# Decode step of two attention and MLP layers: weights of 448 rows on all 128 partitions, two more K/V slots, last rows in moving form

## The chip, the cores and the metric

The kernel runs on one core of one Trainium2 chip. The metric is the device time of one execution, in microseconds (us). Three runs of the kernel before took 310.23, 316.7 and 318.95 us (median 316.7). The profile below is of one more execution, of 309.65 us.

## The reference

Eight rows x (448 numbers each, one token per batch entry) go through attention, MLP, attention, MLP, each with a layer norm ahead and a residual sum behind. Both rounds use the same weights and the same cache.

```python
W = min(4096, max(256, Sk // 4))                  # 1024 of 4096 positions
q = (layernorm(x) @ wq).reshape(8, 1, 16, 256)    # wq 448 x 4096, 16 heads of 256
k = repeat(k_cache[:, :, Sk - W:, :], 2)          # 8 K/V heads, each for 2 query heads
v = repeat(v_cache[:, :, Sk - W:, :], 2)
o = softmax(q @ k.T * 256 ** -0.5) @ v
x = x + o @ wo                                    # wo 4096 x 448
x = x + silu(layernorm(x) @ w1) @ w2              # w1 448 x 1792, w2 1792 x 448
```

All tensors are bf16. K and V of the window are 67.1 MB, the four weights 10.5 MB (wq and wo 3.67 MB each, w1 and w2 1.61 MB each).

## The kernel before, in words

Everything is loaded once, on SyncE's one DMA queue, in this order: x, wq (four DMAs of 112 rows), the eight K tiles of batch 0, wo, the eight V tiles of batch 0, w1, w2, and then K and V of batch 1, 2 and so on. A K or V tile is 512 KB and fills one of R = 27 slots of SBUF. A batch needs 16 slots and holds them through both layers. A load into a used slot waits on SyncE until layer 2 of an earlier batch has read it; since the queue is in order, all later loads wait behind it.

At the start the eight rows are normalised together and multiplied by wq (L468, 128 matmuls), which gives the queries of layer 1 for all batches. Then the batches go one after the other. Layer 1 of a batch: VectorE transposes each K tile in place (L839, two instructions a tile), TensorE makes scores (L570, four 32-column tiles of the array side by side), VectorE takes maxima (L576) and ScalarE exponentials into e_sb (L590), TensorE turns them (L595) and ScalarE copies them to pT_sb (L599). The values of the first four K/V heads come from pv_rows (L627, V is the moving operand), are copied to o_sb (L634), turned (L636) and scaled (L640). Those of the last four heads come from pv_cols: V is the stationary operand and two columns of pT_sb move (L656, 16 matmuls a head); L662 scales them. wo_part multiplies by wo in four rows of one PSUM bank (L699).

The function chain then does what lies between the two attentions of one batch, for a single row: fold copies the four partial rows to rowb (L713) and turns them into a column (L715), the layer norm sums (L670, L678), the 56 matmuls with w1 (L468), silu (L729 to L738), w2 (L741), fold again, the second norm (L748) and wq (L755), then the query of layer 2 (L760 to L553). The matmuls of L706 multiply by zeros and only keep TensorE occupied. Layer 2 uses the same K and V. While chain runs for batch b, layer 1 of batch b+1 is also being worked on. After the last batch final_wo and final_rows do wo and the last MLP for all eight rows at once (L468 with 8 columns, L781 to L808).

The order of instructions on each engine is not written by hand: every step is a task with a listed duration, and a scheduler (Plan.schedule) places the tasks by the longest chain behind them, with the rates given for the DMAs. Waits follow from the buffers' names: a task waits for the writers of what it reads and for the readers of what it overwrites, and a PSUM bank counts as one buffer.

With 448 = 4 x 112, the weights wq and w1 and the columns of x use partitions 0 to 111 in four chunks. In the second kernel they use three chunks of 128 rows and a last one of 64.

Of the kernel before, what the change touches and what calls it, by code (L numbers as in the profile page):

```python
# [6 lines left out]
BF16 = mybir.dt.bfloat16  # L7
# [245 lines left out]
def bass_interleave_layers__sliding_block_cached__dense_activation_silu__decode_kernel(  # L253
# [12 lines left out]
    CP = D // KC  # L266
# [4 lines left out]
    R = 27  # L271
# [27 lines left out]
    mT = [sb(f"mT{i}", [P, 32], F32) for i in range(2)]  # L299
# [4 lines left out]
    o_sb = [sb(f"o_sb{i}", [P, DH], BF16) for i in range(3)]  # L304
# [37 lines left out]
    C_XF = 256  # L342
    C_W1 = 32
# [33 lines left out]
    dve(lambda e: e.memset(ones_b[:], 1.0), [], ["ones_b"], 0.1, -99)  # L377
    dve(lambda e: e.memset(rowb[:], 0.0), [], ["rowb"], 0.15, -99)
# [4 lines left out]
    dve(lambda e: e.memset(xb0[:, :, NB:NB + 1], 1.0), [], ["xb0_1"], 0.08, -99)  # L383
# [521 lines left out]
```

## Time and profile before

| | |
|---|---|
| profiled execution | 309.65 us |
| its span, first to last instruction | 307.8 us |
| time around the span | 1.85 us |
| busy: TensorE matmul, VectorE, ScalarE, GpSimd | 218.9, 147.1, 69.3, 10.5 us |
| DMA | 77.68 MB, 73% of what the 16 engines' span holds |
[...]

PE is TensorE's matmuls, PEld its weight loads, DVE VectorE, ACT ScalarE, SPq SyncE with its DMA issues. An arrow "bank<-slot,qbd" is output from inputs.

### The profile page before, as it was taken

Reading aid. Unit: us, or ns where it says so; the run is one execution under the profiler, and the core shown is the slowest. Engines: PE = TensorE matmul, PEld = TensorE weight load, DVE = VectorE, ACT = ScalarE, POOL = GpSimd, SP = SyncE. Lnnn points to the kernel's source line nnn. Section 1 sums busy time; section 2 is a strip of 40 time slices with the busy share of each in tenths; the row PEclk is TensorE's granted clock in tenths of the full one; section 3 lists DMA queues with packets and bytes.
Section 4 is the critical chain, followed back from the end, with each engine's and each line's share of the span. In section 5 each row is a group of like instructions: output and inputs, shape, how many; then the busy total and the mean of one; then the engine's idle time right before and its main releaser. Section 6 shows DMA issues by size and latency. Waiting matters only on the chain.

```text
span 307.8 us, 9763 instructions
## 1 busy us (share of the span) xinstructions
PE 218.9 (71%) x4402; PEld 126.5 (41%) x4402; DVE 147.1 (48%) x436; ACT 69.3 (23%) x203; POOL 10.5 (3%) x22
## 2 busy tenths in 40 slices
PE   1052357675798778868796968788878897888683
PEld 1051113433454456345434634554455345443363
DVE  6049400158317934882487269427744674111113
ACT  2000100121312240423132223312231224022111
POOL 0002000000000000010001000000000000000000
PEclk9999999998675999799579999985799579657555
DMA  7999999999995199949955994999099919000000
GB/s 202 292 399 385 372 348 266 333 405 352 372 402 192 21 355 404 317 138 372 402 192 169 377 398 155 308 399 371 21 317 403 365 35 321 5 2 2 0 5 1
DMA packets 49977, 78.30 MB, mean 254 GB/s; under 512 B 2176, under 2 KB 40848, under 8 KB 49488
## 3 DMA queue, kind: packets, MB, share of 16 engines
q1 hardware_dynamic: 49936, 77.68, 73.3%
q8 instruction: 34, 0.56, 0.8%
q14 instruction: 7, 0.06, 0.0%
HBM read 77.67 MB, written 0.01 MB: 252 GB/s over the span
## 4 chain that ended last, share of the span: by engine, by line
PE 53%; DVE 14%; SPq 13%; ACT 10%; DMA 5%; issue 5%; ACTq 0%
PE bank L627 9%; SPq L444 8%; PE bank L468 7%; PE bank L570 6%; PE bank L699 5%; DVE slot L839 5%; PE bank L755 5%; DMA w_sb<-in_B_w_dram 5%; PE bank L656 4%; PE bank L706 4%; PE bank L741 4%; SPq L432 2%; ACT e_sb L590 2%; DVE qbd L553 2%; PE bank L595 2%
## 5 line engine op out<-in xcount | busy, mean ns | idle before, releaser
L839 DVE STREAM_TRANSPOSE slot<-slot 128x512 uint32<-128x512 uint32 x128 | 81.9, 686 | 9.4 <-DMA slot<-in_A_k_cache_dram 9.2
L570 PE MATMUL bank<-slot,qbd 128*8 128x256 bf16 x1024 | 41.0, 300 | 19.6 <-DVE mseg L576 8.9
L570 PEld LDWEIGHTS bank<-slot,qbd 128*8 128x8 bf16 x1024 | 24.7, 90 | 30.9 <-DVE mseg L576 10.1
L627 PE MATMUL bank<-slot,pT_sb 128*2 128x256 bf16 x768 | 30.6, 304 | 6.8 <-DMA slot<-in_A_v_cache_dram 3.9
L706 PE MATMUL bank<-sel,cols_b 128*128 128x480 bf16 x64 | 27.3, 524 | 2.6 <-DVE vneg L729 2.6
L590 ACT ACTIVATE e_sb<-bank,mb 128x256 bf16<-128x256 f32 x32 | 13.4, 471 | 42.9 <-DVE mb L586 42.8
L627 PEld LDWEIGHTS bank<-slot,pT_sb 128*2 128x2 bf16 x768 | 16.6, 88 | 14.8 <-DMA slot<-in_A_v_cache_dram 5.5
L713 ACT ACTIVATE rowb<-bank 128x448 bf16<-128x448 f32 x16 | 8.7, 544 | 61.9 <-PE bank L699 44.8
L699 PE MATMUL bank<-wo_sb,oT 128*1 128x448 bf16 x256 | 21.4, 435 | 1.6 <-issue 0.9
L656 PE MATMUL bank<-pT_sb,slot 128*128 128x2 bf16 x512 | 17.6, 164 | 4.2 <-issue 2.9
L656 PEld LDWEIGHTS bank<-pT_sb,slot 128*128 128x128 bf16 x512 | 15.3, 98 | 12.3 <-issue 9.9
L755 PE MATMUL bank<-wq_sb,xn 112*1 112x512 bf16 x256 | 20.3, 448 | 0.1
L608 DVE TENSOR_REDUCE l_sb<-bank 128x16 f32<-128x64 f32 x16 | 3.6, 225 | 35.0 <-PE bank L603 26.6
L468 PE MATMUL bank<-xbt,w_sb 112*128 112x32 bf16 (+1 forms) x504 | 16.7, 182 | 3.2 <-ACT xbt L722 1.9
L576 DVE TENSOR_REDUCE mseg<-bank 128x1 f32<-128x256 f32 x32 | 13.1, 413 | 11.3 <-PE bank L570 11.3
L662 DVE TENSOR_TENSOR oT<-bank,rl_sb 128x4 bf16<-128x4 f32 x32 | 5.2, 163 | 25.6 <-PE bank L656 25.6
L538 POOL TENSOR_TENSOR qbd<-q1s,mask 128x256 bf16<-128x256 bf16 x16 | 9.8, 613 | 215.4 <-PE bank L570 192.9
L640 DVE TENSOR_TENSOR oT<-bank,rl_sb 128x16 bf16<-128x16 f32 x24 | 5.0, 208 | 25.4 <-PE bank L636 24.8
L468 PEld LDWEIGHTS bank<-xbt,w_sb 112*128 112x128 bf16 x504 | 15.1, 102 | 4.0 <-ACT xbt L722 2.4
L760 ACT ACTIVATE rowb<-bank,rstd 128x512 bf16<-128x512 f32 x16 | 11.0, 687 | 20.1 <-PE bank L755 20.1
L634 ACT ACTIVATE o_sb<-bank 128x256 bf16<-128x256 f32 x24 | 9.2, 384 | 27.5 <-PE bank L627 27.2
L595 PE MATMUL bank<-ident,e_sb 128*128 128x128 bf16 x64 | 7.2, 243 | 11.1 <-ACT e_sb L590 11.1
(117 smaller groups left out, 195.5 us busy)
## 6 DMA issues: line engine op xcount, KB each, us to landing
slot<-in_A_k_cache_dram SPq DMA_DIRECT2D x64, 512.0 KB, 11.0
slot<-in_A_v_cache_dram SPq DMA_DIRECT2D x64, 512.0 KB, 8.6
wq_sb<-in_A_wq_dram SPq DMA_DIRECT2D x4, 896.0 KB, 9.7
wo_sb<-in_A_wo_dram SPq DMA_DIRECT2D x1, 3584.0 KB, 26.9
w_sb<-in_B_w_dram SPq DMA_DIRECT2D x2, 1568.0 KB, 16.4
qbd<-in_A_x_dram SPq DMA_DIRECT2D x1, 7.0 KB
out_dram<-e_sb SPq DMA_DIRECT2D x1, 7.0 KB
```

The costliest lines, as they stand in the source:

```text
L444: dma(lambda e: e.dma_start(slots[s][:, :].rearrange("v (j n) -> v j n", j=4), src.rearrange("j (v uh) d -> v j (uh d)", uh=2)), [("slot", ...
L468: fns.append(lambda e, o=o, i=i: e.matmul(bank[bank_i][:, col + (o - outs[0]) * n:col + (o - outs[0] + 1) * n], lhs(o, i), rhs(i).broadcas ...
L570: fns.append(lambda e, cb=cb, par=par, j=j, kvh=kvh, kv=kv: e.matmul(bank[sc][32 * j:32 * j + 8, k2 * 256:(k2 + 1) * 256], qbd[qi][:, kvh, ...
L576: dve(lambda e: e.tensor_reduce(mseg[layer][:, k2:k2 + 1], bank[sc][:, k2 * 256:(k2 + 1) * 256], AX.X, ALU.max, negate=True), bk(sc), [("m ...
L590: act(lambda e, k2=k2: e.activation(e_sb[ei][:, k2, :, :].rearrange("p uh (jj ul) -> p uh jj ul", ul=4), bank[sc][:, k2 * 256:(k2 + 1) * 2 ...
L595: pe([lambda e, c=c: e.matmul(bank[lb][:].bitcast(BF16)[:, c * P:(c + 1) * P], e_sb[ei][:, c // 2, c % 2, :], ident[:, :], is_transpose=Tr ...
L627: fns.append(lambda e, q=q, uh=uh, j=j, vv=vv: e.matmul(bank[ob][32 * j:32 * j + 2, c0:c0 + DH], pT_sb[ei][:, k2 * 2 + uh, j * 8 + 2 * q:j ...
L656: fns.append(lambda e, a=a, q=q, uh=uh: e.matmul(bank[vb][:, c0 + 2 * a:c0 + 2 * a + 2], vs[:, (2 * q + uh) * DH + a * P:(2 * q + uh) * DH ...
L699: fns.append(lambda e, i=i, c=c, kvh=kvh: e.matmul(bank[XB][32 * c:32 * c + 1, 0:D], oT1[:, i % 2, i // 2:i // 2 + 1], wo_sb[:, i * D:(i + ...
L706: pe([lambda e: e.matmul(bank[YB][:, 32:512], zero_b.broadcast_to([P, P]), sel[:].rearrange("p c m -> p (c m)")[:, 0:480], start=False, st ...
L755: pe([lambda e, j=j, c=c, k2=k2, wb=wb: e.matmul(bank[wb][32 * j:32 * j + 1, :], xn[0:CP, c:c + 1], wq_sb[0:CP, c, (4 * k2 + j) * 512:(4 * ...
L839: dve(lambda e, v=v: e.transpose(v, v), [("slot", s)], [("slot", s)], 0.67, prio, "KT")
```

## The change

It does five things. The names are those of the code.

1. wq and w1 lie on all 128 partitions: three chunks of 128 rows, and the last 64 rows split by columns, the first half of the columns on partitions 0 to 63 and the second half on 64 to 127. wq is loaded by three DMAs of 128 partitions and two of 64, w1 by one of 128 and two of 64. x gets a fifth column (KX = 5): its last 64 numbers stand once on the lower and once on the upper partitions, with zeros on the other half, and x_c picks the column that fits the half. The number of matmuls with weights stays; a fold takes five small matmuls for four.
2. The SBUF that this frees, and some more, goes to two more slots (R = 29). e_sb is one buffer for both layers (two before), and o_sb two for three: both value passes of layer 2 share one.
3. pv_cols moves 32 columns of pT_sb where it moved two; only two of the 32 results are read.
4. final_wo and the last w2 are in moving form: the eight rows are stationary, the weights move with 448 columns in four tiles of the array, and fold8 (a copy on ScalarE and five matmuls) adds and turns the four partial results, twice.
5. The scheduler's DMA rates follow (w1 260 to 350, w2 280 to 350, wq 305 to 400 GB/s).

```diff
-    CP = D // KC
+    CT = D - (KC - 1) * P
+    KX = KC + 1
...
-    R = 27
+    R = 29
...
-    wq_sb = sb("wq_sb", [P, KC, HD], BF16)
-    wo_sb = sb("wo_sb", [P, NCH * D + 16], BF16)
-    w1_sb = sb("w1_sb", [P, KC, F], BF16)
-    w2_sb = sb("w2_sb", [P, FC * D + 16], BF16)
+    wq_sb = sb("wq_sb", [P, 3 * HD + HD // 2], BF16)
+    wo_sb = sb("wo_sb", [P, NCH * D], BF16)
+    w1_sb = sb("w1_sb", [P, 3 * F + F // 2], BF16)
+    w2_sb = sb("w2_sb", [P, FC * D], BF16)
...
-    e_sb = [sb(f"e_sb{i}", [P, 2, 2, P], BF16) for i in range(2)]
-    pT_sb = [sb(f"pT_sb{i}", [P, 4, 32], BF16) for i in range(2)]
+    e_sb = sb("e_sb", [P, 2, 2, P], BF16)
+    pT_sb = [sb(f"pT_sb{i}", [P, 5 - i, 32], BF16) for i in range(2)]
...
-    o_sb = [sb(f"o_sb{i}", [P, DH], BF16) for i in range(3)]
+    o_sb = sb("o_sb", [P, 2, DH], BF16)
...
     def load_wq():
-        for c in range(KC):
-            dma(lambda e, c=c: e.dma_start(wq_sb[0:CP, c, :], A_wq[c * CP:(c + 1) * CP, :]),
-                [("wq", c)], CP * HD * 2, "wq%d" % c, rate=305e3)
+        for c in range(KC - 1):
+            dma(lambda e, c=c: e.dma_start(wq_sb[:, c * HD:(c + 1) * HD], A_wq[c * P:(c + 1) * P, :]),
+                [("wq", c)], P * HD * 2, "wq%d" % c)
+        for h in range(2):
+            dma(lambda e, h=h: e.dma_start(wq_sb[CT * h:CT * h + CT, 3 * HD:],
+                                           A_wq[3 * P:, h * (HD // 2):(h + 1) * (HD // 2)]),
+                [("wq", 3 + h)], CT * HD, "wq%d" % (3 + h))
 
     def load_w1():
-        dma(lambda e: e.dma_start(w1_sb[0:CP, :, :], B_w1.rearrange("(c p) n -> p c n", p=CP)),
-            ["w1"], D * F * 2, "w1", rate=260e3)
+        dma(lambda e: e.dma_start(w1_sb[:, 0:3 * F].rearrange("p (c n) -> p c n", n=F),
+                                  B_w1[0:3 * P, :].rearrange("(c p) n -> p c n", p=P)), [("w1", 0)], 3 * P * F * 2, "w1",
+            rate=350e3)
+        for h in range(2):
+            dma(lambda e, h=h: e.dma_start(w1_sb[CT * h:CT * h + CT, 3 * F:],
+                                           B_w1[3 * P:, h * (F // 2):(h + 1) * (F // 2)]),
+                [("w1", 1 + h)], CT * F, "w1%d" % h)
...
+    def w_l(w, width, o, c, n=P):
+
+        if c < KC - 1:
+            return w[:, c * width + o * n:c * width + (o + 1) * n]
+        o = o * n % (width // 2)
+        return w[:, (KC - 1) * width + o:(KC - 1) * width + o + n]
+
+    def x_c(x, c, h=0):
+
+        return x[:, c] if c < KC - 1 else x[:, c + h]
+
+    def turned(dst, row, m):
+
+        out = [(dst[:, c], row[m, c * P:(c + 1) * P]) for c in range(KC - 1)]
+        return out + [(dst[CT * h:CT * h + CT, KC - 1 + h], row[m, (KC - 1) * P:D]) for h in range(2)]
+
+    def proj(bank_i, col, outs, n_out, w, width, x, n, fresh=True):
 
         fns = []
-        wide = n == 1
-        n = CW if wide else n
         for o in outs:
-            for i in ins:
-                fns.append(lambda e, o=o, i=i: e.matmul(
-                    bank[bank_i][:, col + (o - outs[0]) * n:col + (o - outs[0] + 1) * n], lhs(o, i),
-                    rhs(i).broadcast_to([rhs(i).shape[0], CW]) if wide else rhs(i),
-                    start=(fresh and i == ins[0]), stop=(i == ins[-1]), skip_group_check=not fresh))
+            for c in range(KC):
+                xc = x_c(x, c, 2 * o // n_out)
+                fns.append(lambda e, o=o, c=c, xc=xc: e.matmul(
+                    bank[bank_i][:, col + (o - outs[0]) * n:col + (o - outs[0] + 1) * n], w_l(w, width, o, c),
+                    xc if xc.shape[-1] == n else xc.broadcast_to([P, n]),
+                    start=(fresh and c == 0), stop=(c == KC - 1), skip_group_check=not fresh))
...
-        oi = layer + k2
+        oi = layer
...
-        c0 = (0 if j % 2 == 0 else C_Q) + 4 * j
+        c0 = (0 if j % 2 == 0 else C_Q) + 32 * (j - j % 2)
+        pf = pT_sb[ei][:].rearrange("p c n -> p (c n)")
...
-                        bank[vb][:, c0 + 2 * a:c0 + 2 * a + 2],
+                        bank[vb][:, c0 + 32 * a:c0 + 32 * a + 32],
                         vs[:, (2 * q + uh) * DH + a * P:(2 * q + uh) * DH + (a + 1) * P],
-                        pT_sb[ei][:, k2 * 2 + uh, j * 8 + 2 * q:j * 8 + 2 * q + 2],
+                        pf[:, (2 * k2 + uh) * 32 + 8 * j + 2 * q:(2 * k2 + uh) * 32 + 8 * j + 2 * q + 32],
...
-        pe([lambda e, c=c: e.matmul(bank[YB][0:CP, c:c + 1], rowb[:, c * CP:(c + 1) * CP], ones4,
-                                    start=False, stop=True, skip_group_check=True) for c in range(KC)],
+        pe([lambda e, o=o, r=r: e.matmul(o, r, ones4, start=False, stop=True, skip_group_check=True)
+            for o, r in turned(bank[YB][:, 0:KX].unsqueeze(2), rowb, slice(0, P))],
...
-        dve(lambda e: e.tensor_scalar(xn[0:CP, :], xbt[0:CP, :], nmean[0:CP, 0:1], None, op0=ALU.add),
-            ["xbt", "nmean"], ["xn"], 0.2, prio, "xn")
+        dve(lambda e: e.scalar_tensor_tensor(out=xn[:], in0=xb0[:, :, NB], scalar=nmean[:, 0:1], in1=xbt[:],
+                                             op0=ALU.mult, op1=ALU.add), ["xbt", "nmean"] + XB1, ["xn"], 0.23, prio, "xn")
...
-                bank[wb][32 * j:32 * j + 1, :], xn[0:CP, c:c + 1],
-                wq_sb[0:CP, c, (4 * k2 + j) * 512:(4 * k2 + j + 1) * 512],
-                start=(c == 0), stop=(c == KC - 1), tile_position=(0, 32 * j), skip_group_check=True)
+                bank[wb][32 * j:32 * j + 1, :], x_c(xn[:].unsqueeze(2), c, k2),
+                w_l(wq_sb, HD, 4 * k2 + j, c, 512),
+                start=(c == 0), stop=(c == KC - 1), skip_group_check=True)
...
+    x8 = bank[YB][:, 0:KX * NB].rearrange("p (c b) -> p c b", b=NB)
+
+    def fold8(prio):
+        act(lambda e: e.activation(rowb[:, 0:D], bank[XB][:, 0:D], ACTF.Copy), bk(XB), ["rowb"], 0.54, prio, "rowb8")
+        pe([lambda e, o=o, r=r: e.matmul(o, r, sel8, start=False, stop=True, skip_group_check=True)
+            for o, r in turned(x8, rowb, slice(0, P))], ["rowb", "sel8"], bk(YB), (140, 1), prio, "fold8")
...
-        pe(proj(XB, C_XF, range(KC), range(16 * k2, 16 * k2 + 16), wo_l, lambda i: oT2[:, i % 2, i // 2, :], NB,
-                fresh=False), [(("oT2", b), 2 * h) for b in range(NB) for h in range(4 * k2, 4 * k2 + 4)] + WO_R, bk(XB), (NB, 1), prio, "wo8")
+            pe(lambda e: e.matmul(bank[YB][:, 0:KX * NB], identf, x2s[:].rearrange("p c b -> p (c b)"),
+                                  start=True, stop=True),
+               [("q1s", 0)] + [("x2s", b) for b in range(NB)], bk(YB), (500, 1), prio, "xinit8")
+        pe([lambda e, i=i: e.matmul(
+            bank[XB][32 * (i % 4):32 * (i % 4) + NB, 0:D], oT2[:, i % 2, i // 2, :], wo_sb[:, i * D:(i + 1) * D],
+            start=(i < 4), stop=(i >= NCH - 4), skip_group_check=True) for i in range(16 * k2, 16 * k2 + 16)],
+           [(("oT2", b), 2 * h) for b in range(NB) for h in range(4 * k2, 4 * k2 + 4)] + WO_R, bk(XB), (D, 4), prio,
+           "wo8")
...
-        pe(proj(XB, C_XF, range(KC), range(FC), w2_l, lambda i: hT8[:, i * NB:(i + 1) * NB], NB, fresh=False),
-           H8 + W2_R, bk(XB), (NB, 1), prio + 0.2, "w28")
-        act(lambda e: e.activation(xob[0:CP], xp, ACTF.Copy), bk(XB), ["xbt8"], 0.22, prio + 0.3)
-        ops = bank[YB][:].bitcast(BF16)
-        pe([lambda e, c=c: e.matmul(ops[0:NB, c * CP:(c + 1) * CP], xob[0:CP, c, :], ident[0:CP, 0:CP],
-                                    is_transpose=True, start=True, stop=True) for c in range(KC)],
-           ["xbt8", "ident"], bk(YB), (CP, 1), prio + 0.3)
-        dve(lambda e: e.tensor_copy(orow, ops[0:NB, 0:D]), bk(YB), B8, 0.3, prio + 0.3)
+        pe([lambda e, f=f: e.matmul(
+            bank[XB][32 * (f % 4):32 * (f % 4) + NB, 0:D], hT8[:, f * NB:(f + 1) * NB], w2_sb[:, f * D:(f + 1) * D],
+            start=(f < 4), stop=(f >= FC - 4), skip_group_check=True) for f in range(FC)],
+           H8 + W2_R, bk(XB), (D, 4), prio + 0.2, "w28")
+        fold8(prio + 0.2)
```

## Rows read from the trace of the kernel before

**Rows 1.** The page's chain that ended last, shares of the span by engine
```profile
PE 53%; DVE 14%; SPq 13%; ACT 10%; DMA 5%; issue 5%; ACTq 0%
```
**Rows 2.** Windows: busy us per engine, granted clock, DMA share, GB/s (wq, K, V, w1)
```profile
4.00:14.00 10.00, 0.48 (x12) 0.40 (x12) 3.35 (x21) 0.83 (x3) 0.00 (x0) 1.00 1.02 292
16.00:24.00 8.00, 4.78 (x161) 4.53 (x161) 4.47 (x8) 0.50 (x1) 0.15 (x1) 1.00 1.02 408
...
38.00:46.00 8.00, 3.69 (x58) 1.27 (x62) 0.62 (x4) 0.38 (x1) 0.00 (x0) 1.00 1.09 349
49.00:55.00 6.00, 3.68 (x49) 1.84 (x46) 0.70 (x4) 0.85 (x3) 0.00 (x0) 1.00 1.06 238
```
**Rows 3.** Timeline of the start: start, length, instruction, idle before and releaser
```profile
16.37 3.56 PE L468 MATMUL bank<-xb,wq_sb 112*128 112x9 bf16 x128 [10.80 <-DMA wq_sb<-in_A_wq_dram]
...
56.95 1.68 PE L468 MATMUL bank<-ones_b,w_sb 112*128 112x32 bf16 x56 [2.44 <-DMA w_sb<-in_B_w_dram]
...
61.76 0.96 PE L741 MATMUL bank<-w_sb,hT 128*1 128x448 bf16 x14
```
**Rows 4.** Windows of single stretches; the third number from the right is the granted clock
```profile
143.80:147.20 3.40, 2.60 (x71) 1.72 (x71) 0.67 (x4) 0.00 (x0) 0.00 (x0) 1.00 1.02 401
147.20:157.40 10.20, 8.95 (x117) 4.14 (x118) 6.26 (x15) 2.34 (x7) 0.00 (x0) 0.50 1.04 385
...
177.90:186.60 8.70, 6.54 (x114) 3.61 (x113) 6.47 (x16) 2.58 (x9) 0.00 (x0) 1.00 1.04 386
...
123.30:126.60 3.30, 2.97 (x17) 0.65 (x17) 2.85 (x7) 0.96 (x4) 0.00 (x0) 0.50 1.03 384
...
283.70:307.70 24.00, 14.95 (x362) 10.55 (x362) 5.73 (x22) 3.41 (x11) 0.00 (x0) 0.50 0.01 2
```
**Rows 5.** Groups by line and form: busy us, mean ns, idle before and releasers
```profile
L839 DVE STREAM_TRANSPOSE slot<-slot 128x512 uint32<-128x512 uint32 x128 | 81.9, 686 | 9.4 <-DMA slot<-in_A_k_cache_dram 9.2
...
L656 PE MATMUL bank<-pT_sb,slot 128*128 128x2 bf16 x512 | 17.6, 164 | 4.2 <-issue 2.9 <-DMA slot<-in_A_v_cache_dram 1.0 <-DVE oT L662 0.3
```
**Rows 6.** Timeline: pv_cols' first group and chain's second norm, two of seven batches
```profile
173.74 0.98 PE L656 MATMUL bank<-pT_sb,slot 128*128 128x2 bf16 x32
...
186.30 0.23 DVE L748 TENSOR_SCALAR xn<-xbt,nmean 112x4 bf16<-112x4 bf16 x1
...
261.46 0.73 PE L656 MATMUL bank<-pT_sb,slot 128*128 128x2 bf16 x22
...
276.80 0.23 DVE L748 TENSOR_SCALAR xn<-xbt,nmean 112x4 bf16<-112x4 bf16 x1
```
**Rows 7.** Timeline: w1 matmuls with 32 columns
```profile
180.51 0.85 PE L468 MATMUL bank<-xbt,w_sb 112*128 112x32 bf16 x28
```
**Rows 8.** Timeline of the exponentials and the value copies in one batch
```profile
168.79 0.40 PE L595 MATMUL bank<-ident,e_sb 128*128 128x128 bf16 x4 [1.24 <-ACT e_sb L590]
...
169.40 0.83 ACT L590 ACTIVATE e_sb<-bank,mb 128x256 bf16<-128x256 f32 x2
...
172.66 0.82 ACT L634 ACTIVATE o_sb<-bank 128x256 bf16<-128x256 f32 x2 [1.41 <-PE bank L627]
...
173.05 0.20 PE L636 MATMUL bank<-ident,o_sb 128*128 128x8 bf16 x2
```
**Rows 9.** Timeline of a wo part, a fold and the last rows
```profile
266.21 1.66 PE L699 MATMUL bank<-wo_sb,oT 128*1 128x448 bf16 x16
...
267.92 0.54 ACT L713 ACTIVATE rowb<-bank 128x448 bf16<-128x448 f32 x1 [6.73 <-PE bank L699]
...
269.22 0.17 ACT L722 ACTIVATE xbt<-bank 112x4 bf16<-112x4 f32 x1 [0.76 <-PE bank L715]
...
296.30 1.87 PE L468 MATMUL bank<-oT,wo_sb 128*128 128x8 bf16 x64 [0.32 <-DVE oT L640]
...
303.16 1.65 PE L468 MATMUL bank<-qbd,w_sb 128*128 128x8 bf16 x56 [2.45 <-DVE qbd L799]
```
**Rows 10.** Timeline of VectorE: four K transposes behind the second norm
```profile
186.75 2.48 DVE L839 STREAM_TRANSPOSE slot<-slot 128x512 uint32<-128x512 uint32 x4
```

More of the change, by code (lines that the diff above doesn't have):

```diff
@@ L382, in bass_interleave_layers__sliding_block_cached__dense_activation_silu__decode_kernel @@
         dve(lambda e, q=q: e.memset(ones4[32 * q:32 * q + 1, :], 1.0), [("ones4", 4)], [("ones4", q)], 0.08, -98)
-    dve(lambda e: e.memset(xb0[:, :, NB:NB + 1], 1.0), [], ["xb0_1"], 0.08, -99)
+    dve(lambda e: e.memset(xb0[:, :, NB:NB + 1], 0.0), [], [("xb0_1", 0)], 0.08, -99)
+    for i, (p0, p1, c0, c1) in enumerate(((0, P, 0, KC - 1), (0, CT, KC - 1, KC), (CT, P, KC, KX))):
+        dve(lambda e, p0=p0, p1=p1, c0=c0, c1=c1: e.memset(xb0[p0:p1, c0:c1, NB:NB + 1], 1.0), [("xb0_1", 0)],
+            [("xb0_1", i + 1)], 0.08, -98)
+    XB1 = [("xb0_1", i) for i in range(4)]
     for q in range(4):
@@ L472, in proj @@
         return fns
+    ones_w = ones_c.broadcast_to([P, P])
     def stats8(xp, reads, prio):
-        sq = sq8[0:CP]
-        act(lambda e: e.activation(sq, xp, ACTF.Square), reads, ["sq8"], 0.25, prio)
-        dve(lambda e: e.tensor_copy(sqh8[0:CP, 0], sq), ["sq8"], [("sqh8", 0)], 0.17, prio)
-        dve(lambda e: e.tensor_tensor(sqh8[0:CP, 1], sq, sqh8[0:CP, 0], ALU.subtract),
+        sq = sq8[:]
+        act(lambda e: e.activation(sq, xp, ACTF.Square), reads, ["sq8", "rowb"], 0.25, prio)
+        dve(lambda e: e.tensor_copy(sqh8[:, 0], sq), ["sq8"], [("sqh8", 0)], 0.17, prio)
+        dve(lambda e: e.tensor_tensor(sqh8[:, 1], sq, sqh8[:, 0], ALU.subtract),
@@ L677, in stat_s2 @@
         s1, s2 = bank[bi][:, 0:1], bank[bi][:, 1:2]
-        pe([lambda e, c=c: e.matmul(s2, xbt[0:CP, c:c + 1].broadcast_to([CP, P]), xbt[0:CP, c:c + 1],
+        pe([lambda e, c=c: e.matmul(s2, x_c(x_t, c).broadcast_to([P, P]), x_c(x_t, c),
                                     start=(c == 0), stop=(c == KC - 1)) for c in range(KC)],
@@ L689, in x_init @@
     def x_init(b, prio):
-        pe(lambda e: e.matmul(bank[YB][:, 0:KC], ident[0:CP, :], xb0[0:CP, :, b], start=True, stop=True),
+        pe(lambda e: e.matmul(bank[YB][:, 0:KX], ident[:, :], xb0[:, :, b], start=True, stop=True),
            ["ident", "xb0"], bk(YB), (KC, 1), prio, "xinit")
@@ L704, in keep @@
     def keep(n, prio, after=None):
-        pe([lambda e: e.matmul(bank[YB][:, 32:512], zero_b.broadcast_to([P, P]),
-                               sel[:].rearrange("p c m -> p (c m)")[:, 0:480],
+        pe([lambda e: e.matmul(bank[YB][:, C_W1:512], zero_b.broadcast_to([P, P]),
+                               sel[:].rearrange("p c m -> p (c m)")[:, 0:512 - C_W1],
                                start=False, stop=True, skip_group_check=True) for _ in range(n)],
@@ L725, in chain @@
         for o0, o1 in ((0, 4), (4, 8), (8, 11), (11, 14)):
-            pe(proj(YB, C_W1 + o0 * CW, range(o0, o1), range(KC), w1_l, lambda i: xbt[0:CP, i:i + 1], 1, fresh=False),
+            pe(proj(YB, C_W1 + o0 * CW, range(o0, o1), FC, w1_sb, F, x_t, CW, fresh=False),
                ["xbt"] + W1_R, bk(YB), (CW, 1), prio, "w1")
```

162 lines of the change are left out of this document (74 added, 88 removed).

## Prediction

> **What bounds the kernel now.** I read the chain that ended last first, and look for the engine with the largest share: TensorE has 53%, VectorE and ScalarE 14% and 10%, the DMAs 5% and SyncE 13% [rows 1]. The last two stand together at the start, so there are three stages to price apart. At the start the queue of DMAs is the bound. In the windows of the first 60 us the reader should compare GB/s at a DMA share that is full throughout: wq comes at 292, w1 at 238, but K at 408 and V at 349 [rows 2]. The timeline shows who waits: the first matmuls with wq (10.80 us) and the first with w1 (2.44 us) [rows 3]. In the middle nothing waits for a load. VectorE's K transposes waited 9.4 us for DMAs in all and pv_cols 1.0 us [rows 5], both of it in the start (the first K and V tiles). There each batch costs its own chain through TensorE, VectorE and ScalarE, and the clock matters: stretches of 10 us at 0.50 stand beside others of the same work at 1.00 [rows 4]. The last 24 us run at 0.50 with no DMA to speak of [rows 4]; that is the third stage.
>
> **Loads of wq and w1: -5.0 us.** wq is 3.67 MB, at 292 GB/s 12.6 us [rows 2]. After the change 3.15 MB of it go to 128 partitions with rows of 8 KB, as K's tiles do with 4 KB: at 408 that is 7.7 us. The other 0.52 MB go in two loads to 64 partitions, a shape that the trace does not have. Bounds: 408 (1.3 us) and 238, the slowest load shown (2.2 us). I take 292, since a load to fewer than 128 partitions is nearest to the 112-row wq: 1.8 us. wq saves 12.6 - 9.5 = 3.1 us (2.7 to 3.6). w1 is 1.61 MB: 6.7 us at 238. Its 1.38 MB on 128 partitions come as several pieces a partition, as V does: 349, 3.9 us; the 0.23 MB in halves at 238: 1.0 us. Saved 1.8 us, up to 2.8 at 408 throughout. Sum 4.9, rounded 5.0 (4.5 to 6.4). It all lies on the path: V tiles and w1 queue behind wq without a gap, and the first w1 matmuls start when w1 lands [rows 3]. Three more DMA issues cost nothing while SyncE runs ahead of the wire; where that cover is gone they are three issues of under a microsecond. w2 lands after w1 unchanged; its matmuls start 4.8 us behind the first with w1 [rows 3], which its 1.61 MB at 349 (4.6 us) just fills.
>
> [...] No row here has a 64-partition load.
>
> **pv_cols with 32 columns: -4.0 us.** The instructions cost nothing more: 32 matmuls with two columns take 0.98 us [rows 6], 31 ns each, and the w1 matmuls with 32 columns take 0.85 us for 28, 30 ns [rows 7]. What may change is the clock. It fell while pv_cols and the wo matmuls between them ran in four of the seven batches behind the first: the window 143.80 to 147.20 ran at 1.00, the 10.2 us behind it at 0.50 [rows 4]. The work from pv_cols' first group to the second norm took 12.56 us where no fall came (173.74 to 186.30) and 15.34 in the longest of the seven (261.46 to 276.80) [rows 6]; the four with such a fall took 13.40, 14.74, 14.04 and 15.34, together 7.3 us more than four of the shortest. With 16 times the columns at the same pace the array is busier just there. Against it: right behind the w1 matmuls, which have 32 columns already, the clock held in one batch (177.90 to 186.60) and fell in another, at 0.50 from 123.30 to 126.60 [rows 4]. So a fall may only come some us later. Ends: 0 and -8 (the 7.3, and some of the wq stage that followed at 0.50). I take the half.
>
> **Two more slots: 0.** No transpose or matmul of the middle waits for a load, so earlier loads end no wait. They and the new rates shift the scheduler's order. The nearest price is a group of four K transposes on VectorE, 2.48 us [rows 10], put ahead of or behind something urgent: once, in either direction.
>
> **One e_sb, two o_sb: +0.5 us.** Each adds a wait. e_sb: in the batch shown the second exponentials start at 169.40 and the first layer's turns are over at 169.19 [rows 8], so this wait costs 0 as ordered; queued behind it on ScalarE is the copy of pT. o_sb: the second value copy of layer 2 must now wait until the first is turned. Two copies run back to back at 172.66 for 0.82 us, and the next turn is issued at 173.05 [rows 8]. If that turn is not moved forward, the copy starts behind it (173.25) and not at 172.66 or 173.10, 0.2 to 0.6 us later; with a semaphore each way up to 1.0. pv_cols writes the same PSUM bank that this copy reads, so TensorE's queue, wo included, waits for it. Over seven batches 0 to 7 us. I take 0.5 in all, since a turn can go earlier between the value matmuls.
>
> **Last rows: +1.3 us.** Twice 64 matmuls with wo take 1.87 us each and the 56 with w2 1.65 [rows 9]. In moving form 16 take 1.66 us at 0.50 (L699) [rows 9], 14 at that rate 1.45: saved 0.2 + 0.2 + 0.2. Two folds are new. From the start of rowb to the start of xbt is 1.30 us (267.92 to 269.22) [rows 9], twice 2.6, on the path. Net +2.0 at 0.50. With the clock at 1.00 for part of it, the 46 matmuls would take up to half their time, -2.4, so the ends are -0.4 and +2.0; +1.3 since the stage ran at 0.50 throughout [rows 4]. A fold's fifth matmul, the fifth column of x, the memsets and the other xn instruction are within 0.1 us each.
>
> **Sum.** Against the profiled execution of 309.65: -5.0 - 4.0 + 0 + 0.5 + 1.3 = -7.2, 302.5 us. That execution is the fastest of four; the median run is 7 us above it, about as much as the four falls cost, and I put the spread down to where the clock falls. With half of the falls gone the median should lie some 1.5 above its profile: **304 us**.
>
> **Rivals.** (1) The clock falls as before, only elsewhere. For it speaks the fall at 123.3. Then only -3.2 remains, from the median 316.7: 313.5 us. (2) The clock holds throughout, also at the end: -5.0 - 8 - 0.4 = -13.4 from the profile, 296 us. For it: both neighbours of pv_cols, wo and scores, run at 1.00. (3) Slower: o_sb's wait at its full price. The turn stays behind the second layer's values, pv_cols waits 1.0 us in seven batches (+7), and the clock falls meanwhile as now: -5.0 + 7 + 2.0 = +4.0 from the median, 321 us. It ends on the slower side as soon as the wait costs more than 0.45 us a batch. Against it: the scheduler knows this wait and can move the turn. (4) The change doesn't do what it says: the halves are so slow that wq and w1 gain 1 us or none; with the clock's half 309 us. For it only that no such load is in the trace.
>
> **Chances.** Forecast 0.45, (1) 0.22, (2) 0.13, (3) 0.12, (4) 0.08. A measurement of this kernel can tell about 2% from no change. Faster by over 2% (under 310.4) are the forecast, (2) and a part of (4), 0.62; slower (over 323) a third of (3) and a reordering that goes wrong, 0.09; the rest, 0.29, is within 2%. The range 297 to 314 leaves out (3) and half of (2); the forecast's own is 300 to 309.
>
> **What the profile would show.** The wq matmuls at about 13.3 and not 16.37, w1's at about 52; GB/s near 400 up to wq's end but for a dip. Granted clock 1.00 through the wo matmuls behind pv_cols in most batches, first group to second norm under 13 us. No ScalarE wait on L636 of over 0.3 us ahead of the value copy. Two rowb copies in the last 15 us, and from the first of them to the end some 1 to 2 us more. Wrong would make it: a fall in each batch behind the w1 matmuls; pv_cols waiting for ScalarE; a dip to 200 GB/s that eats the load's gain; K transposes ahead of the queries of layer 2.

## The result, and the profile after

The changed kernel took 288.5 us in the median of its first four runs (285.1 to 294.1), 0.922 of before, with an interval of 0.906 to 0.938; in six more runs (a_again, below) 291.8 us, 0.933 [0.921, 0.945]. All ten together have a median of 291.5 us. The kernel before had 315.0 us over the 66 runs that stand beside the experiments. So the gain is 23.5 us, 7.5%. Forecast were 304 us (297 to 314), which is 12.7 us under the 316.7 us that stood ahead of the prediction. Medians here hold all executions, while the ratios leave out those over 1.5% above the fastest of their kernel, and where too few are left no ratio is given.

The profiled execution took 294.11 us, 15.5 us less than the one profiled before; its span is 292.2 us and its mean granted clock 0.899. First the start, windows of the changed kernel (columns as in rows 2) and its timeline:

```profile
4.00:10.00 6.00, 0.48 (x12) 0.40 (x12) 3.46 (x22) 0.84 (x3) 0.00 (x0) 1.00 1.02 429
11.00:13.00 2.00, 0.00 (x0) 0.00 (x0) 0.00 (x0) 0.00 (x0) 0.00 (x0) 1.00 1.03 231
...
45.00:48.00 3.00, 2.24 (x60) 1.49 (x55) 0.49 (x3) 0.00 (x0) 0.00 (x0) 1.00 1.03 400
48.00:51.00 3.00, 1.60 (x19) 0.69 (x15) 0.38 (x2) 1.05 (x4) 0.00 (x0) 1.00 1.08 284
```
```profile
13.89 1.27 PE L476 MATMUL bank<-xb,wq_sb 128*128 128x9 bf16 x42 [8.29 <-DMA wq_sb<-in_A_wq_dram]
...
51.91 1.64 PE L476 MATMUL bank<-xb,w_sb 128*128 128x32 bf16 x56 [1.63 <-DMA w_sb<-in_B_w_dram]
...
56.49 0.74 PE L752 MATMUL bank<-w_sb,hT 128*1 128x448 bf16 x12 [0.28 <-DVE hT L749]
```

(The stretches asked for end before the first and the third of these groups do, so they hold 42 of 128 and 12 of 14 matmuls.) wq now comes at 429 GB/s where it came at 292 [rows 2], and its last 64 rows make a dip to 231. While w1 lands, the traffic is at 284 where it was at 238 [rows 2]. The matmuls with wq start 2.5 us earlier, those with w1 5.0, the first with w2 5.3 (61.76 in rows 3).

The chain that ended last, and the groups of rows 5, in the changed kernel:

```profile
PE 56%; SPq 14%; DVE 13%; ACT 10%; issue 4%; DMA 3%; ACTq 0%; DVEq 0%
...
L865 DVE STREAM_TRANSPOSE slot<-slot 128x512 uint32<-128x512 uint32 x128 | 82.4, 686 | 6.6 <-DMA slot<-in_A_k_cache_dram 6.6
...
L665 PE MATMUL bank<-pT_sb,slot 128*128 128x32 bf16 x512 | 17.3, 178 | 1.7 <-issue 1.4
```

TensorE's share grew from 53% to 56%; that of the DMAs fell from 5% to 3%, and SyncE's went from 13% to 14% [rows 1]. The 32 columns cost pv_cols no time: 17.3 us for 512, 17.6 with two [rows 5].

Next the clock. The page's slices of the span, 40 of them, tell where TensorE was slowed (9 is full speed, 5 half). Of the kernel before, then of the changed one:

```profile
PEclk9999999998675999799579999985799579657555
```
```profile
PEclk9999999779596599997889797988999989999795
```

The profiled execution of before has a mean of 0.839. Of its 506 windows of half a microsecond from 55 us on, 489 read 1.00 or 0.50, so this mean is (1 - 0.839) x 2 = 32% of the span at 0.50; at 0.899 it is 20%. Ten of the 40 slices stand at 5 or 6 before and four in the changed kernel; in the last quarter these are six and one. The stretches from pv_cols' first group to the second norm of a batch, three of seven, and the stage behind the last norm (windows of the changed kernel):

```profile
112.16:123.88 11.72, 10.18 (x216) 5.86 (x214) 8.37 (x24) 2.59 (x9) 0.00 (x0) 1.00 1.05 382
...
200.07:211.71 11.64, 10.12 (x214) 5.84 (x214) 8.50 (x23) 2.59 (x9) 0.00 (x0) 1.00 1.06 377
...
252.47:263.82 11.35, 9.44 (x198) 5.55 (x198) 2.29 (x12) 2.59 (x9) 0.00 (x0) 1.00 0.01 3
...
263.80:274.00 10.20, 6.20 (x131) 3.45 (x134) 2.63 (x9) 3.31 (x9) 0.00 (x0) 1.00 0.01 2
...
284.20:292.20 8.00, 2.67 (x23) 0.94 (x23) 2.04 (x6) 1.05 (x4) 0.00 (x0) 0.50 0.01 3
```

These stretches took 12.56 to 15.34 us before [rows 6]; the seven together are 9.8 us shorter. The last rows, timeline of the changed kernel:

```profile
264.10 1.90 PE L766 MATMUL bank<-wq_sb,xn 128*1 128x512 bf16 x32
...
278.05 0.93 PE L794 MATMUL bank<-wo_sb,oT 128*8 128x448 bf16 x16 [0.32 <-DVE oT L648]
...
280.42 0.54 ACT L784 ACTIVATE rowb<-bank 128x448 bf16<-128x448 f32 x1 [2.27 <-PE bank L794]
...
281.42 0.20 ACT L802 ACTIVATE xbt<-bank 128x40 bf16<-128x40 f32 x1 [0.46 <-PE bank L785]
...
286.41 1.66 PE L822 MATMUL bank<-w_sb,qbd 128*8 128x448 bf16 x14 [2.48 <-DVE qbd L821]
```

The two groups with wo take 0.93 us each at full clock (1.87 before, rows 9), a fold 1.0 us from rowb to xbt (1.30 assumed), and the 14 with w2 1.66 us, as long as the 56 before them.

**How to read the runs.** The clock differs from run to run of one kernel: the changed one took 285.1 us at a mean of 0.937 and 299.9 at 0.859. One slope fitted to 166 runs of these kernels, each about its own kernel's mean, is 1.7 us for 0.01 of clock. With it each kernel also has a time at the same clock of 0.90; what two kernels differ by there isn't the clock. No run set the clock by itself, so these are readings, not proofs.

| kernel | runs | median us | mean clock | us at 0.90 |
|---|---|---|---|---|
| before | 66 | 315.0 | 0.828 | 302.3 |
| b_newend (last rows) | 12 | 310.6 | 0.854 | 301.8 |
| b_cols32 (columns) | 6 | 308.6 | 0.866 | 303.0 |
| b_both (both) | 6 | 305.1 | 0.878 | 300.9 |
| a_c2R27 (two columns, 27 slots) | 6 | 302.3 | 0.850 | 294.4 |
| a_R27 (27 slots) | 6 | 294.2 | 0.916 | 297.0 |
| a_cols2 (two columns) | 6 | 293.6 | 0.886 | 292.1 |
| changed | 10 | 291.5 | 0.912 | 293.4 |

### The profile page after: what moved, and what is told of

The parts are those of the page before. It is cut to its first block, busy times and chain, and to the rows that moved or that the text cites. A ratio compares the mean times of both kernels' runs of the same rounds, so it can differ in the third digit from the quotient of the medians.

```text
span 292.2 us, 9554 instructions
## 1 busy us (share of the span) xinstructions
PE 207.3 (71%) x4291; PEld 117.4 (40%) x4291; DVE 147.0 (50%) x438; ACT 70.3 (24%) x205; POOL 10.5 (4%) x22
## 4 chain that ended last, share of the span: by engine, by line
PE 56%; SPq 14%; DVE 13%; ACT 10%; issue 4%; DMA 3%; ACTq 0%; DVEq 0%
PE bank L635 10%; PE bank L578 10%; SPq L449 8%; PE bank L476 5%; PE bank L766 5%; PE bank L665 5%; DVE slot L865 5%; PE bank L710 5%; DMA w_sb<-in_B_w_dram 3%; PE bank L752 3%; PE bank L603 2%; PE bank L717 2%; ACT e_sb L598 2%; SPq L443 2%; DVE mseg L584 2%
## 5 line engine op out<-in xcount | busy, mean ns | idle before, releaser
L578 PE MATMUL bank<-slot,qbd 128*8 128x256 bf16 x1024 | 43.2, 301 | 16.0 <-DVE mseg L584 8.9
L578 PEld LDWEIGHTS bank<-slot,qbd 128*8 128x8 bf16 x1024 | 22.4, 90 | 29.3 <-DVE mseg L584 10.3
L717 PE MATMUL bank<-sel,cols_b 128*128 128x472 bf16 x64 | 20.5, 406 | 2.6 <-DVE vneg L740 2.6
L710 PE MATMUL bank<-wo_sb,oT 128*1 128x448 bf16 x256 | 18.0, 382 | 1.1 <-DVE oT L671 0.8
L766 PE MATMUL bank<-wq_sb,xn 128*1 128x512 bf16 x256 | 18.6, 425 | 0.1
L665 PE MATMUL bank<-pT_sb,slot 128*128 128x32 bf16 x512 | 17.3, 178 | 1.7 <-issue 1.4
L476 PE MATMUL bank<-xbt,w_sb 128*128 128x32 bf16 (+1 forms) x504 | 15.8, 176 | 2.2 <-ACT xbt L733 1.9
L642 ACT ACTIVATE o_sb<-bank 128x256 bf16<-128x256 f32 x24 | 9.2, 384 | 29.1 <-PE bank L635 25.5
L476 PEld LDWEIGHTS bank<-xbt,w_sb 128*128 128x128 bf16 x504 | 14.4, 97 | 2.9 <-ACT xbt L733 2.5
L771 ACT ACTIVATE rowb<-bank,scal 128x512 bf16<-128x512 f32 x16 | 11.0, 687 | 15.1 <-PE bank L766 15.1
L752 PE MATMUL bank<-w_sb,hT 128*1 128x448 bf16 x112 | 9.6, 432 | 5.0 <-DVE hT L749 5.0
```

The source lines that it names most:

```text
L476: fns.append(lambda e, o=o, c=c, xc=xc: e.matmul(bank[bank_i][:, col + (o - outs[0]) * n:col + (o - outs[0] + 1) * n], w_l(w, width, o, c) ...
L578: fns.append(lambda e, cb=cb, par=par, j=j, kvh=kvh, kv=kv: e.matmul(bank[sc][32 * j:32 * j + 8, k2 * 256:(k2 + 1) * 256], qbd[qi][:, kvh, ...
L665: fns.append(lambda e, a=a, q=q, uh=uh: e.matmul(bank[vb][:, c0 + 32 * a:c0 + 32 * a + 32], vs[:, (2 * q + uh) * DH + a * P:(2 * q + uh) * ...
L710: fns.append(lambda e, i=i, c=c, kvh=kvh: e.matmul(bank[XB][32 * c:32 * c + 1, 0:D], oT1[:, i % 2, i // 2:i // 2 + 1], wo_sb[:, i * D:(i + ...
L717: pe([lambda e: e.matmul(bank[YB][:, C_W1:512], zero_b.broadcast_to([P, P]), sel[:].rearrange("p c m -> p (c m)")[:, 0:512 - C_W1], start= ...
L752: pe([lambda e, f=f: e.matmul(bank[XB][32 * (f % 4):32 * (f % 4) + 1, 0:D], hT[:, f:f + 1], w2_sb[:, f * D:(f + 1) * D], start=(f < 4), st ...
```

## The experiments

**Columns and slots.** Two columns again (a_cols2), 27 slots again (a_R27), both (a_c2R27), and the columns alone in the kernel before (b_cols32; there seven one-column constants share a buffer, for room).

```diff
-                        bank[vb][:, c0 + 32 * a:c0 + 32 * a + 32],
+                        bank[vb][:, c0 + 2 * a:c0 + 2 * a + 2],
...
-    R = 29
+    R = 27
```

> The changed kernel with pv_cols back at two columns; its order of instructions is the changed kernel's, line for line. Theory 1 (the 32 columns hold the clock): it loses most of the 20 us that lie between the two traces' sums and the loads, about +10 us against the changed kernel, near 299 us and 0.95 of before; low-clock time goes from 61 us back towards 100, and the falls come again while pv_cols and the wo matmuls run. Theory 2 (the gain of the middle is the order of instructions that two more slots bring): within 3 us of the changed kernel, about 290 us and 0.925, with low-clock time of some 60 us. The prediction's own price lies between: +4 us.

> The kernel before with 32 columns in pv_cols and nothing else (seven one-column constants share one buffer, which makes room for the zeros behind pT_sb); TensorE's order is that of before. Theory 1: 10 us faster than before, about 0.968, low-clock time well under the 99 us of before. Theory 2: no difference, 0.99 to 1.01. Prediction: -4 us, 0.987.

> The changed kernel with 27 slots, as before; from the fifth batch on the scheduler orders the instructions otherwise. Theory 1: no difference from the changed kernel, about 288 us and 0.92. Theory 2: the last batches lose the short way from the second norm to the next batch's pv_cols (14.1 us, 16 to 18 in the others), 3 to 6 us slower than the changed kernel, 0.93 to 0.94. Prediction: 0, at most 2.5 us.

> The changed kernel with two columns and 27 slots: what is left are the loads, the shared buffers and the last rows. Prediction: -3.2 us against before, 0.990. Theory 1: the same as with two columns and 29 slots, 0.95 to 0.96. Theory 2: the same as with 32 columns and 27 slots, 0.93 to 0.94. If both hold and add up: loads -5.3 and end -2.5, 0.975.

Measured: a_cols2 293.6 us, 0.934 [0.926, 0.941]; b_cols32 308.6 us; a_R27 294.2 us, 0.934 [0.928, 0.941]; a_c2R27 302.3 us, 0.958 [0.950, 0.966]. Neither theory holds alone. Starting from a_c2R27 either part gives 8 to 9 us, which is clear of the noise. The second then gives only 2 to 3, which is not: the intervals overlap with those of the changed kernel (0.906 to 0.945). In the kernel before the columns give 6.4 us. What they act on is the clock: at 0.90 the kernels with 32 columns lie between 0.9 us under and 2.6 over those with two (four pairs of the table), while the mean clock rises by 0.02 to 0.07. The slots act on it too: at 0.90 they are worth 3.6 us with 32 columns and 2.3 with two, so some 6 of the 8.7 us that they give with two columns came with the clock (0.850 to 0.886). Three of the windows of pv_cols to second norm in a_cols2, whose order of instructions is the changed kernel's (the profiled execution is one of 300.5 us, at 0.857):

```profile
166.89:181.02 14.13, 12.76 (x214) 6.33 (x214) 8.36 (x23) 2.59 (x9) 0.00 (x0) 0.64 1.04 374
197.53:211.41 13.88, 13.08 (x214) 6.34 (x214) 8.50 (x24) 2.59 (x9) 0.00 (x0) 0.63 0.97 340
...
256.97:269.02 12.05, 10.72 (x198) 5.70 (x198) 2.30 (x13) 2.59 (x9) 0.00 (x0) 0.86 0.01 3
```

The same 214 matmuls that took 11.64 us at 1.00 take 13.88 at 0.63. All seven such stretches take 94.2 us, and 86.5 in the changed kernel's profile.

**Slots or order.** The scheduler orders the instructions otherwise with 29 slots. The order was written into the kernel as a list, once the other's each way.

```diff
+        for e, p in FORCED.items():
+            mine = [t for t in tasks if t.eng == e]
+            self.order[e] = [mine[i] for i in p]
         self.order["sp"] = sp_next
```

> The changed kernel with its 29 slots, but TensorE, VectorE, ScalarE and GpSimd take the order of instructions of the kernel with 27 slots (fixed in a list). If the order is what two more slots bring: as with 27 slots, 294 us, 0.934. If the earlier loads themselves bring it: as the changed kernel, 288.5 us, 0.922.

> The reverse: 27 slots and the order of instructions of the changed kernel. If the order brings it: 288.5 us, 0.922. If the loads: K transposes or pv_cols wait for a load in most batches, 294 us or more, 0.934 to 0.96.

Measured: a_R29o27 291.6 us, 0.934 [0.926, 0.942]; a_R27o29 297.4 us, 0.946 [0.936, 0.956]. The order of 29 slots is no gain without the slots: VectorE then waits for K tiles. From the view of waits (total us, times, longest), a_R27o29, then the changed kernel and a_R27:

```profile
DVE slot L871 <- DMA slot<-in_A_k_cache_dram: 21.9, 18, 6.6
```
```profile
DVE slot L865 <- DMA slot<-in_A_k_cache_dram: 6.6, 1, 6.6
```
```profile
DVE slot L865 <- DMA slot<-in_A_k_cache_dram: 7.1, 1, 7.1
```

Seventeen waits with 15 us come in that neither the changed kernel nor a_R27 has. The slots with the old order gave 2.6 us of median, too little to tell from none. With 29 slots the old order is as fast as the new one (291.6 and 291.5 us), so the order by itself is worth nothing that shows.

**Last rows.** In the kernel before, final_wo and the last w2 in moving form with fold8 (four chunks of 112; the seven one-column constants share a buffer here too), nothing else; the kernel before against itself, to see how far two medians of one kernel lie apart; and the last rows with the columns.

```diff
-        pe(proj(XB, C_XF, range(KC), range(16 * k2, 16 * k2 + 16), wo_l, lambda i: oT2[:, i % 2, i // 2, :], NB,
...
+            bank[XB][32 * (i % 4):32 * (i % 4) + NB, 0:D], oT2[:, i % 2, i // 2, :], wo_sb[:, i * D:(i + 1) * D],
...
+        fold8(prio)
```

> The kernel before with the last rows in moving form and the two folds, and nothing else. Prediction: +1.3 us at a clock of 0.50 throughout, 1.004 of before. Rival (the four tiles of 448 columns hold the clock at 1.00 where the 8-column matmuls let it fall): -2 to -4 us, 0.99, and of the 24 us of before at 0.50 behind 283.7 some 10 are at 1.00.

> The kernel before against itself. Whatever the theory: 1.00; how far the ratio or the median strays from that is what a run of this length can't tell. Its profile shows, in a second execution, how long the way from the second norm of the last batch to the end is (31.05 us in the first) and how much of it is at 0.50.

> The last rows in moving form alone, a second time. If the -5.3 us are real: 0.98 to 0.99 again, and the way from the last second norm to the end near 29 us, 2 us under before. If they were spread: 0.99 to 1.00.

> The kernel before with the 32 columns and the last rows in moving form. If the parts add up (-7 and -5): 303.5 us, 0.962. What is left to the run with 27 slots (294.2 us, 0.934) is then 9 us; if loads are all that the layout changes it is 5 to 6, and this run is at 299.5 us, 0.95.

Measured: b_newend 310.6 us, 0.984 [0.978, 0.989], and again 310.4 us, 0.982 [0.971, 0.993]; b_again 314.4 us beside 313.7 for the same kernel in the runs next to it; b_both 305.1 us, 0.969 [0.960, 0.978]. The gain of the last rows came twice, 4 to 5 us. From the last second norm to the end the two profiles of before have 31.0 and 31.2 us, those of b_newend 29.1 and 29.1: 2.0 us. The matmuls with wq at the head of that stage, in b_again and in b_newend, and then b_newend's windows behind them:

```profile
281.62 3.58 PE L755 MATMUL bank<-wq_sb,xn 112*1 112x512 bf16 x32
```
```profile
274.64 1.90 PE L752 MATMUL bank<-wq_sb,xn 112*1 112x512 bf16 x32
```
```profile
274.40:282.80 8.40, 5.54 (x118) 2.99 (x118) 2.60 (x9) 2.33 (x7) 0.00 (x0) 1.00 0.01 2
282.80:289.70 6.90, 5.47 (x84) 2.81 (x88) 0.71 (x3) 1.74 (x5) 0.00 (x0) 0.51 0.00 1
289.70:293.10 3.40, 2.14 (x43) 0.95 (x36) 0.23 (x1) 0.97 (x3) 0.00 (x0) 1.00 0.02 5
293.10:303.40 10.30, 4.62 (x87) 2.82 (x84) 3.32 (x12) 1.64 (x5) 0.00 (x0) 0.50 0.00 1
```

The 1.7 us at wq go with the clock: in the first profile of before this group took 3.49 us, and the window 276.80:280.30, which holds nearly all of it, is at 0.50, b_newend's first window above at 1.00. In the stage of the last rows itself one of the two groups with wo got the full clock. The turn of the last exponentials in before and in b_newend, and b_newend's two groups with wo:

```profile
288.25 0.61 PE L595 MATMUL bank<-ident,e_sb 128*128 128x128 bf16 x4 [2.15 <-ACT e_sb L590]
```
```profile
283.55 0.61 PE L592 MATMUL bank<-ident,e_sb 128*128 128x128 bf16 x4 [2.15 <-ACT e_sb L587]
...
288.89 1.29 PE L781 MATMUL bank<-wo_sb,oT 128*8 128x448 bf16 x16 [0.32 <-DVE oT L637]
...
290.63 0.93 PE L781 MATMUL bank<-wo_sb,oT 128*8 128x448 bf16 x16 [0.32 <-DVE oT L637]
```

From that turn to the end of the span (307.8 and 303.5) b_newend takes 19.9 us, 19.6 before. So the rows themselves cost 0.3 us, less than the 1.3 forecast, and the gain lies ahead of them, in work whose order on TensorE hardly changed. Why the clock is higher there (0.854 against 0.828 over the runs) stays open.

**Loads and the rest of the layout.** Four K tiles loaded once more ahead of wq, in the changed kernel and with 27 slots; one DMA in place of the two for the last 64 rows of wq, and of w1 likewise (the second diff has wq's).

```diff
+    for i in range(4):
+        load_k(R - 4 + i, 7, i)
     load_wq()
```
```diff
+        dma(lambda e: e.dma_start(wq_sb[:, 3 * HD:], A_wq[3 * P:, :].rearrange("p (h n) -> h p n", h=2)),
+            [("wq", 3), ("wq", 4)], 2 * CT * HD, "wq3")
```

> The changed kernel, same order of instructions, with four K tiles (2.1 MB) loaded once more than needed, ahead of wq. It measures what time at the start is worth at the end. If the start lies on the path with its full length, as predicted: 2.1 MB at some 410 GB/s, +5.1 us, 294 us. If the later batches absorb a part of it (they would have to wait for something else): +0 to +2 us.

> The changed kernel with 27 slots, its order kept, and four K tiles loaded once more ahead of wq, so that all starts some 5 us later, as in the kernel before. If the loads are what the layout gives: 5.5 us slower than without (294.2), 299.7 us, 0.95, and 5 us remain to the 305 us of the old layout with the two other parts. If the earlier start gives all of the 10 us: 304 us, 0.965.

> The changed kernel, same order of instructions, with the last 64 rows of wq and of w1 each loaded by one DMA to all 128 partitions instead of two DMAs to 64. If a load to 64 partitions is what runs at 229 to 234 GB/s: 0.75 MB at 400 instead, 1.4 us less, the first matmuls with wq at 13.0 instead of 13.9 and those with w1 at 50.5 instead of 51.9, in all 287 us, 0.917. If the short pieces are the cause, nothing changes: the dip stays, 288.5 us.

Measured: a_late 298.1 us (four executions, 290.6 to 307.8); a_R27late 300.9 us, 0.966 [0.937, 0.996]; a_half1 308.7 us, 0.985 [0.974, 0.995]. Both late kernels reach the first second norm 5.6 to 6.0 us later (65.19 for 59.17, 64.83 for 59.27) and are 6.6 and 6.7 us slower in the median, 7.1 and 5.1 at 0.90. So, as far as these wide spreads tell, the start lies on the path with all of its length. The first second norm in the changed kernel and in a_late:

```profile
59.17 0.23 DVE L759 SCALAR_TENSOR_TENSOR xn<-xb,scal,xbt 128x5 bf16<-128x5 bf16 x1
```
```profile
65.19 0.23 DVE L765 SCALAR_TENSOR_TENSOR xn<-xb,scal,xbt 128x5 bf16<-128x5 bf16 x1
```

Between b_both and a_R27 are 10.9 us, so some 4 of them are neither columns nor last rows nor loads. These 4 us go with the clock: a_R27late, which starts as late as b_both, is 4.2 us faster at a mean clock of 0.909 (b_both 0.878), and at 0.90 it isn't (302.1 and 300.9). They also stand only beside the 32 columns: without them the layout gives 8.3 us (b_newend to a_c2R27), which leaves some 2 beyond the loads. The single DMA made things much worse; windows of a_half1 and its wait for wq:

```profile
4.00:10.00 6.00, 0.48 (x12) 0.40 (x12) 3.45 (x22) 0.84 (x3) 0.00 (x0) 1.00 1.01 427
12.00:18.00 6.00, 0.00 (x0) 0.00 (x0) 0.00 (x0) 0.00 (x0) 0.00 (x0) 1.00 1.03 256
```
```profile
PE bank L478 <- DMA wq_sb<-in_A_wq_dram: 22.1, 1, 22.1
```

wq's matmuls started 13.8 us later (27.74 for 13.89), and meanwhile everything together ran at about 256 GB/s. What in the shape of the one DMA makes it slow wasn't tested.

Three candidates for these 4 us were run: separate e_sb and o_sb with 27 slots (a_sep27), and the array's 128 rows given to the old layout by 16 rows that are multiplied by zeros, for wq and w1 (b_rows) and for w1 alone (b_rows2). The diffs have a_sep27 and b_rows2.

```diff
-    e_sb = sb("e_sb", [P, 2, 2, P], BF16)
+    e_sbs = [sb(f"e_sb{i}", [P, 2, 2, P], BF16) for i in range(2)]
...
-        oi = layer
+        oi = layer + k2
```
```diff
+    add("pool", lambda e: e.memset(w1_sb[96:P, :, :], 0.0), writes=["w1"], dur=8.0, prio=-99)
...
-            pe(proj(YB, C_W1 + o0 * CW, range(o0, o1), range(KC), w1_l, lambda i: xbt[0:CP, i:i + 1], 1, fresh=False),
+            pe(proj(YB, C_W1 + o0 * CW, range(o0, o1), range(KC), lambda o, i: w1_sb[:, i, o * P:(o + 1) * P],
+                    lambda i: xbt[:, i:i + 1], 1, fresh=False),
```

> The changed kernel with 27 slots and two e_sb and three o_sb as before, in the order of instructions of the run with 27 slots (294.2 us, 0.934). Prediction: the shared buffers cost 0.5 us (0 to 7), so 293.7 us, 0.932. Rival of the prediction (o_sb's wait at its full price, 1 us in seven batches): 287 us, 0.912.

> The kernel before with 32 columns and the last rows in moving form (305 us, 0.969), its order kept, whose matmuls with w1 and wq in the chains of the third to the last batch use all 128 rows of the array: 16 rows of finite numbers, loaded behind the first 27 tiles, are multiplied by zeros. If more rows hold the clock: mean clock up by 0.02 to 0.04, 300 us, 0.953. If rows don't matter: 305 us, 0.965 to 0.975.

> The kernel before with 32 columns and the last rows in moving form (304.6 us mean, clock 0.878), its order kept, with the 56 matmuls with w1 on all 128 rows of the array in every chain; rows 112 to 127 are zeros. If rows hold the clock: 0.89 to 0.90 and 301 to 302 us. If they don't: 304 to 306 us, clock 0.87 to 0.885.

Measured: a_sep27 296.0 us, 0.947 [0.932, 0.961], so the shared buffers cost nothing that shows. b_rows 312.6 us, inconclusive: its second batch took 42.2 us where b_both's took 33.5, with one wait of 5.0 us for a V tile behind the extra loads to 16 partitions, and one of its six executions took 534.7 us at a clock of 1.00, which nothing here explains. b_rows2 306.6 us, 0.980 [0.973, 0.987], clock 0.885 beside 0.878: no gain from more rows for w1. For wq, b_rows leaves it open.

**Again, and more.**

```diff
+        pe([lambda e: e.matmul(bank[lb][:, 0:256], zero_b.broadcast_to([P, P]),
+                               sel[:].rearrange("p c m -> p (c m)")[:, 0:256],
+                               start=True, stop=True, skip_group_check=True) for _ in range(4)],
...
```

> The changed kernel once more, unaltered, since its first ratio (0.906 to 0.938) is too wide to hold the parts against it. If the two slots are worth what the medians say (5.7 us against 27 slots, 0.934): 288 to 290 us, 0.915 to 0.925. If they are worth nothing, as predicted: 292 to 294 us, 0.93 to 0.935.

> The changed kernel with four more matmuls by zeros (256 columns, results overwritten) in every softmax, between the maxima and the turns, where the profile of the changed kernel still shows the clock fall (134.1, 164.8 and 195.5 us). If TensorE's idle time there is what lets it fall: mean clock over 0.94 and 3 to 5 us less, 284 us, 0.905. If the falls only move elsewhere: 16 times 0.5 us of work at most, 289 to 293 us, 0.92 to 0.935.

Measured: a_again 291.8 us, 0.933, just under the range for slots that are worth nothing, which decides neither way; a_keep 289.8 us, 0.922 [0.907, 0.938]. The matmuls by zeros raised the mean clock to 0.933, and at equal clock cost 2.3 us (295.7 and 293.4, four and ten executions). No version was found that is told apart from the changed kernel as faster.

## Why the prediction was off

The direction was right, the size half. The step that failed is that a higher clock was priced in one place, pv_cols, and kept at or near that of before in every other term: the loads and the layout, the slots and the last rows stand in the sum with their work alone. Put in one after the other, the medians go 315.0, last rows 310.6 (-4.4), columns 305.1 (-5.5), layout with loads and shared buffers 294.2 (-10.9), slots 291.5 (-2.7). Forecast were +1.3, -4.0, -4.5 and 0. Medians of one kernel differ by up to some 3 us by themselves (288.5 and 291.8; before, 313.3 to 315.9).

- **Loads, -5.0.** Right in the sum: 5.3 us at the first w2 matmul, 2.5 each from wq and w1 up to the first w1 matmul where I took 3.1 and 1.8. wq's halves ran at 231 where I took 292, and its 128-row loads at 429 where I took 408. At the end the shift is worth its full length: a start 6.0 and 5.6 us later (a_late, a_R27late) cost 6.6 and 6.7 us in the median.
- **pv_cols, -4.0 (0 to -8).** Right in mechanism, and between its ends or at them in each setting (-5.5, -6.4, -8.2, -2.1, the last not told apart from none): no gain to speak of at equal clock, all of it through the clock. What in the 32 columns holds the clock isn't shown.
- **One e_sb, two o_sb, +0.5.** Right: no cost. ScalarE's value copy did wait for the turn, 8 times, 3.6 us in all and 1.7 at most in the changed kernel's view of waits. That is over the 0.3 us named as a sign, but a_sep27, with the buffers apart, is no faster (296.0 beside 294.2 us). Rival (3) is out.
- **Last rows, +1.3.** Wrong sign. For the stage itself the working was 1.0 too high (+0.3): the two groups with wo took 1.29 and 0.93 us where 1.66 each was taken, and a fold 1.0 where 1.30 was (in the changed kernel), while w2's took 1.66 where 1.45 was. The step "+1.3 since the stage ran at 0.50 throughout" took the clock of before as given, and the kernel as a whole got 4.4 us shorter, all of it ahead of the stage.
- **Two more slots, 0.** The step "no transpose or matmul of the middle waits for a load, so earlier loads end no wait" does not carry its conclusion, and the clock was left out. In a kernel whose order is computed from the loads, waits need not show: a_R27o29 shows 15 us of waits that the order for 27 slots avoids. How much the slots give (2.7 or 8.7 us) depends on the columns; only the 8.7 is clear of the noise, and by the table 2.3 of it is at equal clock. That hidden waits are what these 2.3 us were isn't shown. (Of the 9.4 us that I put down to loads for the K transposes, the row has 9.2.)
- **No term at all** stood for the 4 us that the layout gives beyond its loads beside 32 columns. They go with the clock. Shared buffers, and rows of the array for w1, show no gain; rows for wq and the order that the layout and its rates bring weren't separated, and why the clock is higher stays open.
- **The median.** The profiled 309.65 us of before lies 5.4 us under the median of 66 runs; I had added 1.5. The priced parts came to 7.2 us; the rest of the 12.7 was the guess that the new median would lie nearer to its profile. So it is in part luck that the forecast reached half of the gain.

In sum: the mean clock rose from 0.828 to 0.912, by the slope of 1.7 us for 0.01 some 14 of the 23.5 us, where the sum had 4; and 9 us remain at equal clock, 5 to 7 of them the loads. That is a reading, since no run set the clock by itself. Of the rivals, (2), the clock held throughout, came nearest (296), though the clock still falls, only for shorter.

## What to carry to other kernels

Where TensorE bounds a kernel and its clock moves, take the clock of several runs, not of one profile, and price every part twice: its work at equal clock and what it may do to the clock elsewhere. No waits for a buffer in a scheduled kernel doesn't mean that more buffers are worth nothing; force the new order onto the old buffers to see the waits. Here a last piece of 64 rows was better loaded by two DMAs than by one for both halves (a_half1 308.7 us, the changed kernel 291.5).

## What the runs showed of the hardware beyond that

TensorE sometimes pauses in the middle of a group with nothing in the profile that releases it. Timeline of a_R27, and of the changed kernel:

```profile
110.17 0.32 PE L665 MATMUL bank<-pT_sb,slot 128*128 128x32 bf16 x6
111.40 0.41 PE L665 MATMUL bank<-pT_sb,slot 128*128 128x32 bf16 x10 [0.91 <-issue]
```
```profile
144.06 0.58 PE L665 MATMUL bank<-pT_sb,slot 128*128 128x32 bf16 x16 [1.38 <-issue]
```

In eight of the traces there are 47 such pauses. Six of them are in before and three in the changed kernel, and each of these nine ends 1.36 to 1.54 us behind the end of a packet of 16,384 bytes on the instruction queue (the one before 144.06 ended at 142.54). They add up to 4.8 us in before, 7.2 in a_R27, 6.7 in a_c2R27, 5.7 in a_R29o27, and 2.0 and 2.4 in the changed kernel, 2.8 in a_cols2. That is in favour of the order of 29 slots. But a_R29o27, with 5.7 us of pauses, takes as long as the changed kernel (291.6 and 291.5), which speaks against the pauses being what the slots gained. That they are the loading of code is argued from the coincidence in time and wasn't tested. The two shown cost TensorE 0.91 and 1.38 us.
